# Row maxima of two heads reduced by one VectorE instruction out of two neighbouring PSUM banks, and banks shared out by index

## The chip, the cores and the metric

The kernel runs on one core of a Trainium2 chip. The metric is the time of one execution on the device in microseconds (us); for the kernel before it is the median of three runs. A core has five engines that matter here: TensorE (PE in the profile, with its weight loads as PEld), VectorE (DVE), ScalarE (ACT), GpSimd (POOL) and SyncE (SP), which issues DMAs. Each works off its own queue of instructions in order and waits on semaphores of the others. Matmul results go to PSUM, which has eight banks of 128 partitions by 512 fp32 values; a matmul here fills at most one bank, and the bank can be written again when its last reader is done.

## The reference

One transformer layer in fp32 on 2048 rows of 512, without masking:

```python
# layernorm(x) = (x - mean) / sqrt(var + 1e-5)
qkv = layernorm(x) @ wqkv                 # 512 x 1536, 32 heads of 16
p = softmax(q @ k.T * 16 ** -0.5)         # per head, 2048 x 2048
h = x + (p @ v) @ wo
out = h + silu(layernorm(h) @ w1) @ w2    # w1: 512 x 1792, w2: 1792 x 512
```

## The kernel before, in words

Every large product in it is made of three matmuls with a high and a low part of each factor (`product`, L129 to 136). The 2048 rows of x are four blocks of 512 (`NB`), and attention goes over 32 items (`ITEMS`): one block of queries by four heads. The program has these stages.

1. *Projections by block* (L649 to 693). Each block projects one group of 128 columns of k and of q (`project_qk`), then four tiles of v (`project_v`); layernorm and transposes (`turn_x`) of the next block lie between. The results `ps_qk` are scaled on ScalarE (`ks`, `sh`) with a low part `sl` on VectorE (block 0, L541) or GpSimd (L538); `ps_v` is copied to `va` by ScalarE, and a transpose `ps_tr` is read by ScalarE (`xth`) and then by VectorE (`xtl`).
2. *The rest of the q and k columns* (L717 to 731), 24 products, numbered n from -4 to 19.
3. *Attention* (`scores`, `values`): per group of 128 keys and four heads four score matmuls `ps_s`, four exps on ScalarE (`pt`, L423) and four value matmuls into the bank `pv`. A score that is issued ahead of its stage takes a bank of another kind, as in `begin_scores` (L699) and `some_scores` (L984).
4. After each block of queries its output projection (`output`, L1019) and its MLP (`mlp`, L974): the first product in 14 steps f (L996 to 1005), with SiLU on ScalarE (`g`) and its two halves (`gh`) on ScalarE and GpSimd; then the second (`second`, L954) in 14 steps over four accumulators `ps_acc`, at whose end VectorE adds the residual (`ot`, L971). The last block's is written out apart.

The exponent needs a row maximum for each head and query beforehand. `maximum` (L259) makes a piece of it: one matmul of 128 queries by 512 keys (48 rows deep, as q and k lie there as high and low parts) into a bank, and one VectorE `tensor_reduce` with max to a single column (L271). That is 64 per item and 2048 in all. They are put into the program as fillers. In attention one lies beside each score. Elsewhere they come as bursts (`burst`, L393), in the middle of products: `BESIDE_V`, `BESIDE_V1`, `BESIDE_A` and `BESIDE_A1` give the counts and places in stages 1 and 2; `BESIDE_T` (L712) those of the last two products ahead of attention; `BURSTS_1` has six in most steps of the first MLP product, `BURSTS_2` has 16, 15 and 13 bursts of four in the second; `MORE` puts three beside an output projection, and `last_scores` two behind the last scores. Burst elements alternate between heads with j = 0 and j = 1 (`at["half"]`), which lie on SBUF partitions 0 to 47 and 64 to 111; such matmuls stand on different rows of the PE array, and in the trace the two start 3 to 4 ns apart. The next pair starts 0.22 us later.

All instructions keep the program's order on their engine (`mm`, `pin`, `act`, `dve` and so on). So the order of the work is written by hand, and what a tile framework decides is the semaphores, and, for PSUM, which bank of a pool a tile gets: the pool hands out a bank that has become free. The pools are opened by stage with `open_banks`: sm=5 and st=3 in stage 1 (L428), sm=6, st=1 and su=1 in stage 2 (L714), and from attention on st=4, three pools of one bank that `sm` goes through in a ring, and `pv` (L735). Products take from `st` (stage 2: `st` and `su` by turns), maxima from `sm`. A burst of six in stage 1 takes one more from `st` (L682); a burst in the MLP takes `pv`, which is free there, and in the first product two of `st` (L1004, L1009).

Of the kernel before, what the change touches and what calls it, by code (L numbers as in the profile page):

```python
# [20 lines left out]
P = 128  # L21
# [51 lines left out]
BESIDE_V = [(0, 0), (0, 4, 4, 4)], [(4, 4), (4, 4, 4, 4)], [(6, 6), (6, 6, 6, 5)]  # L73
# [15 lines left out]
def attention_mlp_kernel(ctx: ExitStack, tc: tile.TileContext, x, wqkv, wo, w1, w2, out):  # L89
# [50 lines left out]
    small = ctx.enter_context(tc.tile_pool(name="small", bufs=3))  # L140
    banks = {}

    def open_banks(scope, n, **sizes):

        for kind, bufs in sizes.items():
            banks[kind] = scope.enter_context(tc.tile_pool(name=f"ps_{kind}{n}", bufs=bufs, space=PSUM))

    def bank(name, kind="st", dtype=F32):
        pool_of = banks[kind]
        if isinstance(pool_of, list):  # L150
            pool_of.append(pool_of.pop(0))
            return pool_of[-1].tile([P, 512], dtype, tag=pool_of[-1].name, name=name)
        return pool_of.tile([P, 512], dtype, tag=kind, name=name)
# [50 lines left out]
    def turn(src, dst_h, dst_l, kind="st"):  # L204

        ps = bank("ps_tr", kind).rearrange("p (c n) -> p c n", n=P)
# [52 lines left out]
    def maximum(i, kb, qt, a, j, ps=None):  # L259

        piece = piece_of(i, a)
        n = 1 if i == LAST else 2
        if piece not in mx:
            mx[piece] = small.tile([P, 64], F32, name="mx", bufs=RING + 1)[:, :32 * n].rearrange(
                "p (j a q k) -> p j a q k", j=2, a=n, k=4)
            left[piece] = 32 * n
        if ps is None:
            ps = bank("ps_m", "sm")
        mm(ps, qs[i % RING][64 * j:64 * j + 48, a, qt * P:qt * P + P],
           ks[i % RING][64 * j:64 * j + 48, a, kb * 512:kb * 512 + 512], start=True, stop=True)  # L270
        pin(nc.vector.tensor_reduce(mx[piece][:, j, a % n, qt, kb:kb + 1], ps, axis=AX.X, op=ALU.max))  # L271
        left[piece] -= 1
        return left[piece] == 0
# [31 lines left out]
    def place_max(piece):  # L305

        i, a = piece
        ns = split.pop(piece)
        n = ns.shape[1]
        ps = bank("ps_n", "sm", F16)  # L310
# [47 lines left out]
    def one_max(half=None, ps=None):  # L358

        i = next_item()  # L360
        if i == ITEMS:
            return
        if half is None:
            half = at["half"]
            at["half"] = 1 - half
        if at["blocks"]:

            i = min(range(2), key=lambda n: (todo[n, half] or todo[n, 1 - half] or [(n, KC)])[0][1])
        elif not todo[i, half] and 64 * (i + 2) <= at["ready"] and KC * i - at["next"] > 12:

            i += 1
        half = half if todo[i, half] else 1 - half
        at["done"] += 1
        block = todo[i, half].pop(0)
        piece = piece_of(i, block[3])
        found_all = maximum(*block, ps)

        finish_rest()
        if found_all:
            steps = due_at(piece)  # L380
            g = at["group"]
            if g is None or g + 1 in marks:
                soon(steps, place_max, piece)
                finish_max(piece, g is not None)
                return
            late.setdefault(at["step"] + steps, []).append(piece)
            if steps == WAIT:
                unfinished.append(piece)
                found_at["step"] = at["step"]
            else:  # L390
                finish_max(piece, False)

    def burst(n, *more):  # L393
        for ps in more:
            one_max(ps=ps)
        for _ in range(n - len(more)):
            one_max()
# [16 lines left out]
    def scores(g, k, kind="st"):  # L414

        i = g // KC
        a, j, c = head(g, k)
        assert piece_of(i, a) in placed
        ps = bank("ps_s", kind)
        mm(ps, ks[i % RING][64 * j:64 * j + 64, a, c * P:(c + 1) * P], qs[i % RING][64 * j:64 * j + 64, a, :],  # L420
           start=True, stop=True)
        pts[g, k] = pt_tile("pt")
        act("activation", pts[g, k], ps, AF.Exp, scale=qk_f)  # L423


    with ExitStack() as pa:
        pb = pa.enter_context(ExitStack())
        open_banks(pb, 0, sm=5, st=3)  # L428
# [46 lines left out]
        def measure_rest():  # L475
            n = sum(PIECES)
            ps = bank("ps_sq", "sm")
# [31 lines left out]
        def measure(meanwhile):  # L509

            ps = bank("ps_sq")
# [11 lines left out]
        def project_qk(b, n, beside={}, scale=False, kind="st"):  # L523
# [3 lines left out]
            ps = bank("ps_qk", kind)  # L527
# [19 lines left out]
        def project_v(b, t):  # L547
            ps = bank("ps_v")
# [22 lines left out]
        def idle(n):  # L571
            ps = bank("ps_i")
# [3 lines left out]
        def turn_high(b, t):  # L576
            ps = bank("ps_tr", "sm").rearrange("p (c n) -> p c n", n=P)
# [13 lines left out]
        def first_products(t, *chunks):  # L591
            if t == len(ps_vs):
                ps_vs.append(bank("ps_v", "st" if t < 3 else "sm"))
# [120 lines left out]
        open_banks(pa, 1, sm=6, st=1, su=1)  # L714

        pools.append(ctx.enter_context(tc.tile_pool(name="bp0", bufs=EARLY, side="right")))
        for g in range(1, NG // 2):  # L717
            for m, (b, key) in enumerate([(b, 1) for b in range(NB)] + [(b, 0) for b in range(NB)]):
# [10 lines left out]
                project_qk(b, 2 * g + key, beside, True, "su" if n % 2 else "st")  # L729
# [74 lines left out]
    def divide_part(part, pvs, o_t, kind="st"):  # L804
        ps = bank("ps_q", kind).rearrange("p (t n) -> p t n", n=P)
# [12 lines left out]
    def turn_part(part, o_t, kind="st", engine="act"):  # L818
        ps = bank("ps_o", kind)
# [134 lines left out]
    def second(b, acc, f, gh, gl, inserts={}):  # L954
        w2h, w2l = ws.pop(("w2", f))
        while f == 0 and len(acc) < 4:
            acc.append(bank("ps_acc"))
# [16 lines left out]
    def mlp(b):  # L974
# [13 lines left out]
        def last_scores():  # L988
# [3 lines left out]
            if b < 2:  # L992
                burst(2)

        gates = []
        for f in range(FC):  # L996
# [3 lines left out]
            ps = bank("ps_w1")  # L1000
# [3 lines left out]
                  {6: lambda: burst(n, pv, bank("ps_m"), bank("ps_m"))} if n else {})  # L1004
# [4 lines left out]
        inserts = {SPAN_2 * (n + 1) // BURSTS_2[b]: lambda: burst(4, pv) for n in range(BURSTS_2[b])}  # L1009
# [9 lines left out]
    def output(b, n):  # L1019

        if n < 4:
            ps = bank("ps_wo")
            weave(project_rows(n, ps), {6: lambda: burst(3)} if n < MORE[b] else {})
# [29 lines left out]
    def finish_last(pending):  # L1053
# [5 lines left out]
        ps_rows = [bank("ps_wo", "sm") for _ in range(3)] + [bank("ps_wo")]  # L1059
# [14 lines left out]
        begun = [bank("ps_w1") for _ in range(3)]  # L1074
# [9 lines left out]
        def turn_first(t):  # L1084
            ps = bank("ps_tr", "sm").rearrange("p (c n) -> p c n", n=P)
# [48 lines left out]
        for f in range(FC):  # L1134
# [5 lines left out]
            else:  # L1140
                ps = bank("ps_w", "sm")
# [137 lines left out]
```

## Time and profile before

| what | value |
|---|---|
| median of three runs | 1619.38 us (1619.26 to 1620.99) |
| profiled execution | 1619.58 us |
| its span in the profile | 1617.8 us |
| granted PE clock | 1.00 in every stretch |
| VectorE reduces of `maximum` | 1971 out of `ps_m` and 77 out of `pv` |
| exps | 2048, 609 ns each |

The profile is one execution. A row of the timeline has start and length in us, engine, line of the kernel, operation, output and inputs by the program's names with their shape and type, how many like instructions were put together (x5), and in square brackets the idle time of the engine before it and what ended that. When several instructions are put together, the length runs from the first start to the last end. A row of a group has busy time and mean length in ns, and then the idle time ahead of the group. A row of the chain of waits has start, length and the engine and line that the end hung on. In the table of stretches the columns are the stretch, its length, then busy time and instructions of PE, PEld, DVE, ACT and POOL, the granted clock and the share of the DMA engines.

### The profile page before, as it was taken

Reading aid. Unit: us, or ns where it says so; the run is one execution under the profiler, and the core shown is the slowest. Engines: PE = TensorE matmul, PEld = TensorE weight load, DVE = VectorE, ACT = ScalarE, POOL = GpSimd, SP = SyncE. Lnnn points to the kernel's source line nnn. Section 1 sums busy time; section 2 is a strip of 40 time slices with the busy share of each in tenths; the row PEclk is TensorE's granted clock in tenths of the full one; section 3 lists DMA queues with packets and bytes.
Section 4 is the critical chain, followed back from the end, with each engine's and each line's share of the span. In section 5 each row is a group of like instructions: output and inputs, shape, how many; then the busy total and the mean of one; then the engine's idle time right before and its main releaser. Section 6 shows DMA issues by size and latency. Waiting matters only on the chain.

```text
span 1617.8 us, 28583 instructions
## 1 busy us (share of the span) xinstructions
PE 1603.5 (99%) x10553; PEld 516.2 (32%) x10553; DVE 1408.8 (87%) x2340; ACT 1208.0 (75%) x2397; POOL 443.8 (27%) x696
## 2 busy tenths in 40 slices
PE   9999999999999999999999999999999999999998
PEld 7666422222233322222233322222233322222253
DVE  7899999999998889999998889999987789998421
ACT  5545699999973169999973169999974189999732
POOL 4423455454435201121135201121126101211200
PEclk9999999999999999999999999999999999999999
DMA  5657433334333111111133211111133111100222
GB/s 200 178 160 219 128 98 95 100 113 118 94 76 95 63 51 33 38 45 48 47 77 93 66 51 33 37 49 44 46 78 98 60 51 36 34 12 22 72 85 72
DMA packets 100952, 125.91 MB, mean 78 GB/s; under 512 B 24144, under 2 KB 61072, under 8 KB 100812
## 3 DMA queue, kind: packets, MB, share of 16 engines
q1 hardware_dynamic: 96204, 115.71, 25.4%
q10 hardware_dynamic: 4608, 8.39, 1.9%
q8 instruction: 82, 1.34, 0.3%
q14 instruction: 58, 0.48, 0.1%
HBM read 93.45 MB, written 24.63 MB: 73 GB/s over the span
## 4 chain that ended last, share of the span: by engine, by line
PE 90%; DVE 6%; ACT 3%; issue 1%; DMA 0%; POOL 0%; SPq 0%; DVEq 0%; ACTq 0%
PE pv L96 30%; PE ps_s L96 22%; PE ps_m L96 10%; PE ps_acc L96 9%; PE ps_w L96 8%; PE ps_qk L96 5%; DVE mx L271 4%; ACT pt L110 3%; PE ps_v L96 3%; PE ps_wo L96 2%; PE ps_tr L99 1%; DVE st L113 0%; PE ps_n L99 0%; DVE ot L113 0%; DVE pvs L113 0%
## 5 line engine op out<-in xcount | busy, mean ns | idle before, releaser
L271 DVE TENSOR_REDUCE mx<-ps_m 128x1 f32<-128x512 f32 x1971 | 1233.1, 683 | 51.5 <-PE ps_m L96 21.8
L110 ACT ACTIVATE pt<-ps_s 128x512 f32<-128x512 f32 x2048 | 1010.5, 609 | 152.3 <-PE ps_s L96 133.0
L96 PE MATMUL pv<-pt,va 128*17 128x512 f32 x4096 | 537.5, 598 | 0.6
L96 PE MATMUL ps_s<-qs,ks 64*128 64x512 f16 x2048 | 532.5, 379 | 2.2 <-ACT pt L110 0.5
L96 PE MATMUL ps_m<-ks,qs 48*128 48x512 f16 x1971 | 496.5, 380 | 0.6 <-DVE mx L271 0.2
L96 PEld LDWEIGHTS <-ks 64*128 64x128 f16 x2048 | 149.8, 95 | 548.6 <-issue 434.8
L103 POOL TENSOR_TENSOR ri<-rc,minus 128x16 f32<-128x16 f32 x31 | 90.7, 2927 | 264.4 <-DMA rc<-dn 264.4
L96 PE MATMUL ps_acc<-w,gh 128*128 128x512 f16 x672 | 157.2, 380 | 0.0
L96 PEld LDWEIGHTS pv<-pt,va 128*17 128x17 f32 x4096 | 68.9, 95 | 215.9 <-issue 203.0
L96 PEld LDWEIGHTS <-qs 48*128 48x128 f16 x2048 | 118.7, 94 | 59.6 <-issue 49.2
L110 ACT ACTIVATE g<-ps_w,factors 128x512 f32<-128x512 f32 x56 | 38.5, 687 | 127.6 <-PE ps_w L96 123.3
L96 PE MATMUL ps_w<-hth,w 128*128 128x512 f16 (+1 forms) x472 | 132.9, 369 | 0.0
L96 PEld LDWEIGHTS <-w 128*128 128x128 f16 x708 | 66.2, 98 | 87.9 <-issue 20.8
L96 PEld LDWEIGHTS <-gh 128*128 128x128 f16 x672 | 61.1, 98 | 90.9 <-issue 25.0
L271 DVE TENSOR_REDUCE mx<-pv 128x1 f32<-128x512 f32 x77 | 52.9, 687 | 42.6 <-PE ps_m L96 41.2
L103 POOL TENSOR_TENSOR mx<-mx 128x32 f32<-128x32 f32 x40 | 9.7, 241 | 282.6 <-DVE mx L271 280.8
L96 PE MATMUL ps_w<-htl,w 128*128 128x512 f16 (+1 forms) x236 | 83.9, 368 | 0.0
L103 POOL TENSOR_SCALAR nm<-nm 128x16 f32<-128x16 f32 (+1 forms) x53 | 13.5, 254 | 175.3 <-DVE nm L282 147.8
L110 ACT ACTIVATE ks<-ps_qk,qk_s 128x512 f32<-128x512 f32 x30 | 20.7, 689 | 53.6 <-PE ps_qk L96 51.7
L113 DVE SCALAR_TENSOR_TENSOR gh<-g,factors,gh 128x512 f16<-128x512 f32 x14 | 10.5, 752 | 52.1 <-ACT gh L110 52.1
L103 POOL TENSOR_TENSOR sl<-ks,sh 128x512 f16<-128x512 f32 x30 | 34.8, 1161 | 72.0 <-ACT sh L110 55.6
L96 PE MATMUL ps_qk<-xth,wqk_h 128*128 128x512 f32 x128 | 53.6, 419 | 0.0
(132 smaller groups left out, 1043.1 us busy)
## 6 DMA issues: line engine op xcount, KB each, us to landing
ks<-kd SPq DMA_DIRECT2D x120, 192.0 KB
w<-w1d SPq DMA_DIRECT2D x56, 256.0 KB
w<-w2d SPq DMA_DIRECT2D x56, 256.0 KB
ks<-in_B_w_dram ACTq DMA_DIRECT2D x28, 256.0 KB
w<-in_B_w_dram SPq DMA_DIRECT2D x28, 256.0 KB
qs<-qd SPq DMA_DIRECT2D x128, 48.0 KB
kd<-sh SPq DMA_DIRECT2D x16, 256.0 KB
qd<-sh SPq DMA_DIRECT2D x16, 256.0 KB
```

The costliest lines, as they stand in the source:

```text
L96: tc.keep_in_program_order(nc.tensor.matmul(*a, **k))
L99: tc.keep_in_program_order(nc.tensor.transpose(*a))
L103: tc.keep_in_program_order(getattr(nc.gpsimd, op)(*a, **k))
L110: pin(getattr(nc.scalar, fn)(*a, **k))
L113: pin(getattr(nc.vector, fn)(*a, **k))
L271: pin(nc.vector.tensor_reduce(mx[piece][:, j, a % n, qt, kb:kb + 1], ps, axis=AX.X, op=ALU.max))
```

## The change

PSUM becomes one tile of eight banks, and rings of bank numbers take the place of the pools: `bank` gives the next number of a ring, whether its last user is done or not. `lay_out` sets the rings and starts them anew. The kinds are sm = 0 to 4 and st = 5 to 7 in block 0; from block 1 through stage 2 sm = 0 to 5 and st = 6, 7; in attention st = 0 to 3, sm = 4, 5, 7 and `pv` = 6. The first MLP product alternates between banks 0 and 1, the second has its accumulators in 0 to 3.

In a burst the two heads j = 0 and j = 1 of the same keys, queries and a go into two neighbouring banks, and one `tensor_reduce` reads both: 128x2 out of 128x1024 instead of twice 128x1 out of 128x512. In the MLP the pairs are banks (4, 5), (6, 7) and (2, 3) by turns of a burst, or the first two; elsewhere the next even number of `sm` with its successor. Where no such two are left, two singles are made (6 times). Beside scores, beside the output projection and behind the last scores maxima stay single. 288 reduces are pairs. The last burst of `BESIDE_V` has six instead of five, so that one maximum fewer is left for attention. The matmuls, the instructions of ScalarE and GpSimd and the DMA issues stay the same in number and order, but for some maxima in attention that stand one place further on.

```diff
-BESIDE_V = ... [(6, 6), (6, 6, 6, 5)]
+BESIDE_V = ... [(6, 6), (6, 6, 6, 6)]
...
+    space = psum.tile([P, 8, 512], F32, name="ps")
...
+    def lay_out(**rings):
+        for kind, ring in rings.items():
+            banks[kind] = list(ring)
+    def next_bank(kind):
+        ring = banks[kind]
+        ring.append(ring.pop(0))
+        return ring[-1]
+    def next_pair(kind="sm"):
+        n = next_bank(kind)
+        if n % 2:
+            n = next_bank(kind)
+        assert next_bank(kind) == n + 1
+        return n
+    def bank(kind="st", dtype=F32):
+        ps = space[:, next_bank(kind), :]
+        return ps if dtype == F32 else ps.bitcast(dtype)[:, :512]
...
+        heads = (0, 1) if j is None else (j,)
+        for m, h in enumerate(heads):
+            mm(space[:, n + m, :], qs[i % RING][64 * h:64 * h + 48, a, qt * P:qt * P + P],
+               ks[i % RING][64 * h:64 * h + 48, a, kb * 512:kb * 512 + 512], start=True, stop=True)
+        of = mx[piece][:, :, a % width, qt, kb]
+        if j is None:
+            pin(nc.vector.tensor_reduce(of, space[:, n:n + 2, :], axis=AX.X, op=ALU.max))
+        else:
+            pin(nc.vector.tensor_reduce(of[:, j:j + 1], space[:, n, :], axis=AX.X, op=ALU.max))
...
+    def burst(n, *pairs):
+        for m in range(n // 2):
+            two_max(pairs[m] if pairs else next_pair())
...
-        open_banks(pb, 0, sm=5, st=3)
+        lay_out(sm=range(5), st=range(5, 8))
...
+            if b == 1:
+                lay_out(sm=range(6), st=range(6, 8))
...
-                    n_max = BESIDE_V[b - 1][kind == "v"][n - 2 if kind == "v" else n]
-                    burst(n_max, *[bank("ps_m")] * (n_max > 5))
+                    burst(BESIDE_V[b - 1][kind == "v"][n - 2 if kind == "v" else n])
...
-        open_banks(pa, 1, sm=6, st=1, su=1)
...
-                project_qk(b, 2 * g + key, beside, True, "su" if n % 2 else "st")
+                project_qk(b, 2 * g + key, beside, True)
...
-    open_banks(ctx, 2, st=4, m0=1, m1=1, pv=1, m2=1)
-    banks["sm"] = [banks.pop(f"m{n}") for n in range(3)]
-    pv = bank("pv", "pv")
+    lay_out(st=range(4), sm=(4, 5, 7))
+    pv = space[:, 6, :]
...
             if b < 2:
-                burst(2)
+                singles(2)
 
         gates = []
+        lay_out(st=range(4))
...
-            ps = bank("ps_w1")
+            ps = space[:, f % 2, :]
...
-                  {6: lambda: burst(n, pv, bank("ps_m"), bank("ps_m"))} if n else {})
+                  {6: lambda: burst(n, 4, 6, 2)} if n else {})
...
-        inserts = {SPAN_2 * (n + 1) // BURSTS_2[b]: lambda: burst(4, pv) for n in range(BURSTS_2[b])}
+        inserts = {SPAN_2 * (n + 1) // BURSTS_2[b]: lambda: burst(4, 4, 6) for n in range(BURSTS_2[b])}
...
-            weave(project_rows(n, ps), {6: lambda: burst(3)} if n < MORE[b] else {})
+            weave(project_rows(n, ps), {6: lambda: singles(3)} if n < MORE[b] else {})
```

`two_max` (new) finds the next keys, queries and a that both heads still lack and calls `maximum` with j = None and the pair's first bank.

More of the change, by code (lines that the diff above doesn't have):

```diff
@@ L140, in attention_mlp_kernel @@
     small = ctx.enter_context(tc.tile_pool(name="small", bufs=3))
+    psum = ctx.enter_context(tc.tile_pool(name="psum", bufs=1, space=PSUM))
+    space = psum.tile([P, 8, 512], F32, name="ps")
     banks = {}
[L143 to L153, printed above, removed]
+    def lay_out(**rings):
[14 more added lines that the diff above has]
+        return ps if dtype == F32 else ps.bitcast(dtype)[:, :512]
     ident = const.tile([P, P], F32, name="ident")
@@ L204, in turn @@
     def turn(src, dst_h, dst_l, kind="st"):
-        ps = bank("ps_tr", kind).rearrange("p (c n) -> p c n", n=P)
+        ps = bank(kind).rearrange("p (c n) -> p c n", n=P)
         for c in range(4):
@@ L257, in attention_mlp_kernel, with maximum @@
     mx, left = {}, {}
-    def maximum(i, kb, qt, a, j, ps=None):
+    def maximum(i, kb, qt, a, j, n):
         piece = piece_of(i, a)
-        n = 1 if i == LAST else 2
+        width = 1 if i == LAST else 2
         if piece not in mx:
[L264 to L273, printed above, removed]
+            mx[piece] = small.tile([P, 64], F32, name="mx", bufs=RING + 1)[:, :32 * width].rearrange(
+                "p (j a q k) -> p j a q k", j=2, a=width, k=4)
+            left[piece] = 32 * width
+        heads = (0, 1) if j is None else (j,)
[7 more added lines that the diff above has]
+            pin(nc.vector.tensor_reduce(of[:, j:j + 1], space[:, n, :], axis=AX.X, op=ALU.max))
+        left[piece] -= len(heads)
+        at["done"] += len(heads)
+        finish_rest()
+        if left[piece] == 0:
+            found_maxima(piece)
     def finish_max(piece, urgent):
@@ L356, in due_at, with found_maxima, one_max @@
         return joint - g if joint < start_of(piece) - 2 and joint // KC - 1 not in (-1, *FIRSTS) else WAIT
-    def one_max(half=None, ps=None):
+    def found_maxima(piece):
+        steps = due_at(piece)
+        g = at["group"]
+        if g is None or g + 1 in marks:
+            soon(steps, place_max, piece)
+            finish_max(piece, g is not None)
+            return
+        late.setdefault(at["step"] + steps, []).append(piece)
+        if steps == WAIT:
+            unfinished.append(piece)
+            found_at["step"] = at["step"]
+        else:
+            finish_max(piece, False)
+    def one_max(half=None, n=None):
         i = next_item()
@@ L372, in one_max, with two_max, singles @@
         half = half if todo[i, half] else 1 - half
[L373 to L396, printed above, removed]
+        maximum(*todo[i, half].pop(0), next_bank("sm") if n is None else n)
+    def two_max(n):
+        i = next_item()
+        if i == ITEMS:
+            return
+        both = [next(((t[1], m, t) for t in todo[m, 0] if (*t[:4], 1) in todo[m, 1]), None)
+                for m in (range(2) if at["blocks"] else (i,))]
+        both = min((x for x in both if x), default=None)
+        if both is None:
+            one_max(n=n)
+            one_max(n=n + 1)
+            return
+        _, i, t = both
+        for j in range(2):
+            todo[i, j].remove((*t[:4], j))
+        maximum(*t[:4], None, n)
+    def burst(n, *pairs):
+        assert n % 2 == 0
+        for m in range(n // 2):
+            two_max(pairs[m] if pairs else next_pair())
+    def singles(n):
+        for _ in range(n):
             one_max()
@@ L476, in measure_rest @@
             n = sum(PIECES)
-            ps = bank("ps_sq", "sm")
+            ps = bank("sm")
             mm(ps[:, :n + DC], ones, rest_sq, start=True, stop=True)
@@ L509, in measure @@
         def measure(meanwhile):
-            ps = bank("ps_sq")
+            ps = bank()
             mm(ps[:, :NG], ones, sq, start=True, stop=True)
@@ L571, in idle @@
         def idle(n):
-            ps = bank("ps_i")
+            ps = bank()
             for c in range(n):
@@ L576, in turn_high @@
         def turn_high(b, t):
-            ps = bank("ps_tr", "sm").rearrange("p (c n) -> p c n", n=P)
+            ps = bank("sm").rearrange("p (c n) -> p c n", n=P)
             for c in range(4):
@@ L592, in first_products @@
             if t == len(ps_vs):
-                ps_vs.append(bank("ps_v", "st" if t < 3 else "sm"))
+                ps_vs.append(bank("st" if t < 3 else "sm"))
             for c in chunks:
@@ L1058, in finish_last @@
         act("activation", small.tile([P, 1], F32, name="sw"), ident[:, :1], AF.Silu)
-        ps_rows = [bank("ps_wo", "sm") for _ in range(3)] + [bank("ps_wo")]
+        ps_rows = [bank("sm") for _ in range(3)] + [bank()]
         first = [project_rows(t, ps_rows[t], range(3), stop=False) for t in range(4)]
@@ L1073, in finish_last @@
         found, parts = {}, {}
-        begun = [bank("ps_w1") for _ in range(3)]
+        begun = [bank() for _ in range(3)]
         def add(t):
@@ L1084, in turn_first @@
         def turn_first(t):
-            ps = bank("ps_tr", "sm").rearrange("p (c n) -> p c n", n=P)
+            ps = bank("sm").rearrange("p (c n) -> p c n", n=P)
             for c in range(4):
@@ L1140, in finish_last @@
             else:
-                ps = bank("ps_w", "sm")
+                ps = bank("sm")
                 w1h, w1l = (w.rearrange("p (c n) -> p c n", n=P) for w in ws["w1", f])
```

20 lines of the change are left out of this document (10 added, 10 removed).

## The prediction

> **What bounds the kernel now.** First the page: its busy line, its chain by engine, and the group that the change touches.
>
> ```profile
> PE 1603.5 (99%) x10553; PEld 516.2 (32%) x10553; DVE 1408.8 (87%) x2340; ACT 1208.0 (75%) x2397; POOL 443.8 (27%) x696
> PE 90%; DVE 6%; ACT 3%; issue 1%; DMA 0%; POOL 0%; SPq 0%; DVEq 0%; ACTq 0%
> L271 DVE TENSOR_REDUCE mx<-ps_m 128x1 f32<-128x512 f32 x1971 | 1233.1, 683 | 51.5 <-PE ps_m L96 21.8
> ```
>
> TensorE (PE) is never without work for long, and the maxima on VectorE (DVE) reach the chain only in places. The table of stretches says where: in attention, here 190 to 430 us, ScalarE (ACT) is as full as PE, and VectorE has 10 us to spare.
>
> ```profile
> 190.00:430.00 240.00, 239.51 (x1828) 53.70 (x1826) 229.56 (x373) 239.85 (x490) 116.56 (x166) 1.00 0.39 109
> ```
>
> The change leaves the attention maxima single, so a lighter VectorE buys nothing there. What remains is the stretches beside it, read matmul by matmul. In the first product of the MLP a burst of six maxima comes every 12 matmuls; the timeline shows the first of a run, the second, and the next two:
>
> ```profile
> 487.00 0.39 PE L96 MATMUL pv<-ks,qs 48*128 48x512 f16 x1
> 487.01 0.82 PE L96 MATMUL ps_m<-ks,qs 48*128 48x512 f16 x5
> 487.43 0.69 DVE L271 TENSOR_REDUCE mx<-pv 128x1 f32<-128x512 f32 x1 [1.43 <-PE ps_m L96]
> 488.03 3.07 DVE L271 TENSOR_REDUCE mx<-ps_m 128x1 f32<-128x512 f32 x5
> 490.45 0.39 PE L96 MATMUL pv<-ks,qs 48*128 48x512 f16 x1
> 490.46 1.07 PE L96 MATMUL ps_m<-ks,qs 48*128 48x512 f16 x5
> 494.16 0.39 PE L96 MATMUL pv<-ks,qs 48*128 48x512 f16 x1
> 497.75 0.39 PE L96 MATMUL pv<-ks,qs 48*128 48x512 f16 x1
> ...
> 876.34 20.42 DVE mx L271 x34
> ```
>
> Bursts start 3.45 us apart as long as nothing waits (487.00 to 490.45), then 3.71 and 3.59: the last maximum of a burst waits for a bank that VectorE still reads (1.07 against 0.82 us for the same five matmuls). The last row, from the chain of waits, is the same run of the second MLP: 20.42/34 = 0.60 us from one reduce to the next, and six of them are 3.60. VectorE sets the pace of these runs, by 0.14 us a burst.
>
> **The change part by part.** *One pair's reduce.* No row has 1024 elements, so I bound it: two single reduces take 1.20 from start to start, the dearest case. The cheapest bound has slope alone: a small reduce out of PSUM is
>
> ```profile
> L113 DVE TENSOR_REDUCE qk_s<-ps_sq 128x1 f32<-128x8 f32 x1 | 0.2, 167 | 1.0 <-PE ps_sq L96 1.0
> ```
>
> so 504 more elements cost 683 − 167 = 516 ns, 1.024 ns each. Twice 512 then is 683 + 524 = 1.21 us long; a reduce's start comes 0.08 before its predecessor's end (0.683 against 0.60), so 1.13 apart. An element cost without any fixed part gives 1.05. I take 1.13, which rests on two rows of the same instruction. The Trainium skill, "Perfetto Trace Analysis", section "Optimizing Scalar/DVE Operations", states some 125 ns of overhead per DVE instruction on PSUM and that grouping helps a saturated engine; by it (an estimate) a pair would be 1.20 − 0.125 = 1.07 and the total 1.2 us lower than mine. No run before shows a pair, so I leave it out of the sum.
>
> *Gains.* Six maxima now take 3 × 1.13 = 3.39 of the 3.45. A run of six bursts lost 0.26 + 4 × 0.14 = 0.82; four such runs (two in each of the first two MLPs) lose 3.3. Of that I leave 0.09 at every second burst, since the third pair's bank comes free 0.43 + 2 × 1.13 + 1.21 = 3.90 after a burst's start (0.43 is 487.00 to 487.43), and is wanted at 3.45 + 0.43 (0.82 − 0.39, the last start of the five): with 0.04 for the handover, which is what the reduce at 487.43 took after its matmul's end, about 0.07 to 0.09. **−2.2**. The third MLP has three pairs of bursts with the 0.26 and one 0.22 more: **−0.75**. In the second product every burst of four that follows closely pays the same way:
>
> ```profile
> 549.32 0.74 PE L96 MATMUL ps_m<-ks,qs 48*128 48x512 f16 x3
> 552.05 0.60 PE L96 MATMUL ps_m<-ks,qs 48*128 48x512 f16 x3
> ...
> 101.35 1.10 PE L96 MATMUL ps_m<-ks,qs 48*128 48x512 f16 x6
> ```
>
> 0.14 each, 8 times in the first MLP and 5 in the second, less a tenth to a fifth: **−1.55**. The start of the second projection phase (the last row: 1.10 where six matmuls else take 0.82, then three bursts with 0.12) gives **−0.6**. Gains: 5.1. The 288 reduces that vanish elsewhere lie behind a busy PE and give nothing: VectorE's share falls, the span doesn't.
>
> *Losses: the rings.* A pool gave the bank that was free; a ring gives the next by index. Instruction for instruction PE's order is kept, so I put after's bank numbers on before's times and looked where a bank's last reader ends after the matmul that now wants it. Between projections the ring `st` has two banks where the pool had three.
>
> ```profile
> 28.59 0.39 PE L96 MATMUL ps_qk<-xth,wqk_h 128*128 128x512 f32 x1
> 29.51 0.75 DVE L113 SCALAR_TENSOR_TENSOR sl<-ps_qk,qk_s,sh 128x512 f16<-128x512 f32 x1 [1.06 <-ACT sh L110]
> ...
> 33.55 1.16 POOL L103 TENSOR_TENSOR sl<-ks,sh 128x512 f16<-128x512 f32 x1
> 34.39 0.48 PE L96 MATMUL ps_v<-wv_h,xth 128*128 128x512 f32 x1
> 34.75 0.69 ACT L110 ACTIVATE ks<-ps_qk,qk_s 128x512 f32<-128x512 f32 x1 [1.90 <-POOL sl L103]
> 37.44 0.59 ACT L110 COPY va<-ps_v 128x512 f32<-128x512 f32 x1 [0.34 <-PE ps_v L96]
> 37.59 0.48 PE L96 MATMUL ps_v<-wv_h,xth 128*128 128x512 f32 x1
> ...
> 59.83 1.06 PE L96 MATMUL ps_m<-ks,qs 48*128 48x512 f16 x4
> 60.82 0.66 PE L99 MATMUL ps_tr<-ident,ks 128*128 128x128 f32 x4
> 60.98 0.68 DVE L113 TENSOR_TENSOR xtl<-ps_tr,xth 128x512 fp32r<-128x512 f32 x1
> ```
>
> (1) At 28.59 block 1 begins in bank 6, which block 0 has just filled; VectorE's `sl` reads it till 30.26: **+1.7** with the handover. Behind it on PE stands everything. (2) At 34.39 the first `ps_v` gets bank 7 and waits for ACT's `ks`, to 35.44, itself behind POOL's `sl`; PE is 1.7 late by then, POOL about 1.0, so **+0.6**. (3) At 37.59 the next one waits for ACT's `va`, to 38.03: **+0.5**. (4) At 60.82 a transpose waits for `xtl` of the transpose before, to 61.66: +0.9, less the 0.45 that the burst at 59.83 no longer waits (1.06 against 0.60): **+0.5**. From 40 to 190 us PE has no idle time to absorb these.
>
> (5) Ahead of attention a pair takes banks 4 and 5, and 5 holds a score that ACT has not yet read:
>
> ```profile
> 185.04 0.44 PE L96 MATMUL ps_m<-ks,qs 48*128 48x512 f16 x2
> 185.84 1.08 ACT L110 ACTIVATE pt<-ps_s 128x512 f32<-128x512 f32 x2
> ```
>
> An exp takes 0.6 (two overlap in the 1.08), so the first ends at 186.45; the second matmul of the row above, 0.05 behind its twin (0.44 − 0.39), goes then instead of at 185.09: **+1.4**. (6) The second product's accumulators are the banks 0 to 3 now, where bank 1 holds the last gate:
>
> ```profile
> 534.06 1.68 PE L96 MATMUL ps_acc<-w,gh 128*128 128x512 f16 x7
> 534.06 0.69 ACT L110 ACTIVATE g<-ps_w,factors 128x512 f32<-128x512 f32 x1 [1.15 <-PE ps_w L96]
> 899.55 1.24 PE L96 MATMUL ps_acc<-w,gh 128*128 128x512 f16 x5
> 899.81 0.69 ACT L110 ACTIVATE g<-ps_w,factors 128x512 f32<-128x512 f32 x1 [2.09 <-POOL gh L103]
> 1257.67 3.07 DVE L271 TENSOR_REDUCE mx<-ps_m 128x1 f32<-128x512 f32 x5
> 1258.70 1.89 PE L96 MATMUL ps_acc<-w,gh 128*128 128x512 f16 x8
> 1258.96 0.69 ACT L110 ACTIVATE g<-ps_w,factors 128x512 f32<-128x512 f32 x1 [2.01 <-PE ps_w L96]
> ```
>
> The second accumulator starts three matmuls after the first, 0.64 by (1.24 − 0.39)/4 each, so it waits for ACT's end at 534.75, 900.50 and 1259.65: 0.1, 0.35 and 0.35; in the third the next accumulator's bank 2 waits for the last of three pairs too, which ends 6 × 0.60 − 3 × 1.13 = 0.2 before the six singles do, at 1260.5 instead of 1257.67 + 3.07, and some 0.2 after it is wanted (1258.70 + 6 × 0.21 + the 0.35): **+1.0**. (7) Where attention resumes, a score's bank waits for the residual of the last accumulator:
>
> ```profile
> 949.24 2.26 ACT L110 ACTIVATE pt<-ps_s 128x512 f32<-128x512 f32 x4
> 949.51 0.40 PE L96 MATMUL ps_s<-qs,ks 64*128 64x512 f16 x2
> 949.59 0.74 DVE L113 SCALAR_TENSOR_TENSOR ot<-ps_acc,factors,ot 128x512 f32<-128x512 f32 x1
> ```
>
> 0.8 us, three times. ACT works on four exps till 951.50 there, so the score has time and most is hidden; I charge 0.2 each, and nothing for the scores of the last product: **+0.5**. Uncovered it would be 2.4.
>
> Losses: 1.7 + 0.6 + 0.5 + 0.5 + 1.4 + 1.0 + 0.5 = 6.2. One more maximum ahead of attention and one fewer in it moves no bound: nothing. ACT's, POOL's and SP's orders, and with them every DMA issue, are as before. Sum: 6.2 − 5.1 = +1.1. The profiled execution took 1619.58 (span 1617.80, 1.78 around it), 0.2 above the median of the runs, so **1620.5** beside the median of 1619.4.
>
> **The rivals.**
> *A, forecast*: both halves as worked out. Its own range is 1618 to 1622.6: the sum with the cheapest pair (1.05 to 1.07) and half of wait 5 hidden, up to waits 7 uncovered.
> *B, slower: a pair costs what two singles cost.* At 1.20 three pairs are 3.60, the third pair's bank is free at 0.43 + 2.40 + 1.28 = 4.1, and a run of bursts loses 0.14 or more each as before; the second product's pairs end 2.9 after their start where bank 6 is wanted at 2.82. Gains fall to 0.5: 1619.4 + 6.2 − 0.5 = **1625**. It decides from about 1.16 on; each 0.01 over 1.13 returns some 0.6 us. For it: a bank is held 1.21 where it was held 0.68. Against: 167 ns for eight elements. The Trainium skill, "Perfetto Trace Analysis", section "Optimizing Scalar/DVE Operations", says that an engine which isn't saturated but makes others wait may do better with smaller instructions; by it the bursts lose, which is this rival, and wait 6 of the third MLP is the one place where my sum has that.
> *C, faster: the early waits don't reach the end.* Waits 1 to 3 and 5 (4.2 us) would be made up if PE met waits in 40 to 190 us that end at a fixed time, such as a load, or if ACT still caught up in the start of attention. Then 1620.5 − 4.2 = **1616**. Speaks for: ACT waits 1.90 for POOL at 34.75, so some slack exists. Against: no DMA is in the chain, 0%.
> *D, it isn't done*: pairs fall back on singles. The order of after has 288 reduces fewer and 6 pairs split, so this is small; the time would be that of B.
>
> **How the numbers follow.** A 0.58, B 0.22, C 0.17, D 0.03. A measurement tells 0.2%, 3.2 us, from no change: 1616.1 to 1622.6. Faster: half of C and a little of A, 0.12. Slower: B and D, and the upper tail of A, 0.28. Same: 0.60. The range of 1616.0 to 1625.0 holds A, C's nearer half and B up to its own value.
>
> **What would show it.** The pair's row, 128x2 out of 128x1024: about 1.21 us, 1.13 from one to the next (B: over 1.25). VectorE 1408.8 less 288 × 0.07 (by spacing) to 0.16 (by length), some 1375 us; PE's idle time in the MLP's first products nearly gone, their bursts 3.45 apart. Against that, new gaps on PE at 28.6, 34, 37.6 and 185, with the releasers named above, and each later event shifted by their sum: attention should begin some 4 us later, and the MLPs win about 1.7, 1.2 and 0 back. If the shift at 180 is under 1 us, C is right; if the MLPs win nothing, B is. The forecast fails as a whole if a pair's two matmuls no longer run side by side, 0.22 us each 288 times, which nothing here suggests.

## The result, and the profile after

The changed kernel takes 1622.22 us (median of 17 runs, 1621.98 to 1623.64) against 1619.38 before (17 runs). The ratio is 1.0018 with a 95% interval of 1.001 to 1.0025, so it is 2.8 us slower, just inside the 0.2% that the prediction called no change. The profiled spans differ by the same amount, 1620.6 less 1617.8.

From the page of the kernel after: the busy line, the chain by engine, and the two groups of reduces.

```profile
PE 1600.2 (99%) x10553; PEld 521.3 (32%) x10553; DVE 1392.9 (86%) x2052; ACT 1207.9 (75%) x2397; POOL 442.6 (27%) x696
PE 90%; DVE 5%; ACT 3%; issue 1%; DMA 0%; POOL 0%; SPq 0%; DVEq 0%; ACTq 0%
L287 DVE TENSOR_REDUCE mx<-ps 128x1 f32<-128x512 f32 x1472 | 926.5, 684 | 47.0 <-PE ps L96 18.8
L285 DVE TENSOR_REDUCE mx<-ps 128x2 f32<-128x1024 f32 x288 | 336.1, 1220 | 62.0 <-PE ps L96 61.3
```

A pair takes 1.22 us. VectorE has 15.9 us less work. PE is "busy" 3.3 us less, and that is no gain: matmuls of 0.39 us start 0.22 apart, so the short stalls of before lay under the length of the matmul ahead of them and counted as busy, while the new waits are longer and show as idle time. The page as a whole tells almost nothing of what happened. The view of PE's waits does (what waits, for whom; us in total, times, longest). Of these six releasers the view of the kernel before has only `pt`, with three waits of 0.5 us in all:

```profile
PE ps L96 <- DVE sl L113: 1.6, 1, 1.6
...
PE ps L96 <- DVE ot L113: 1.3, 3, 0.5
PE ps L96 <- ACT pt L110: 1.2, 1, 1.2
...
PE ps L99 <- DVE xtl L113: 0.9, 1, 0.9
...
PE ps L96 <- ACT ks L110: 0.5, 1, 0.5
...
PE ps L96 <- ACT g L110: 0.4, 2, 0.2
```

Those for `sl`, `pt`, `xtl` and `ks` come once each, ahead of attention, those for `ot` at the blocks' ends and those for `g` in the MLPs. (Three waits for `htl`, 0.8 in all, are new too, but the matmuls behind them are as late as those ahead, so they cost nothing.) The timeline of after has the early ones one by one, with one for `va` besides; set each beside the same matmul of before (28.59, 34.39, 37.59, 60.82 and 185.11 us):

```profile
30.68 0.51 PE L96 MATMUL ps<-xth,wqk_h 128*128 128x512 f32 x1 [1.56 <-DVE sl L113]
37.38 0.50 PE L96 MATMUL ps<-wv_h,xth 128*128 128x512 f32 x1 [0.49 <-ACT ks L110]
41.07 0.50 PE L96 MATMUL ps<-wv_h,xth 128*128 128x512 f32 x1 [0.24 <-ACT va L110]
64.88 0.66 PE L99 MATMUL ps<-ident,ks 128*128 128x128 f32 x4 [0.91 <-DVE xtl L113]
190.20 0.37 PE L96 MATMUL ps<-ks,qs 48*128 48x512 f16 x1 [1.21 <-ACT pt L110]
```

The bracket is shorter than the delay, since it counts only from the end of the matmul before; the difference of the starts is what PE lost. Because both kernels run the same matmuls, such a difference can be followed through the whole program, and it is the account of the change. In the table a positive number means that after is later at that matmul.

| matmul | before, us | after, us | later by | step |
|---|---|---|---|---|
| second transpose of block 0 | 8.43 | 8.77 | 0.35 | 0.35, a load of x |
| block 1, first `ps_qk` | 28.59 | 30.68 | 2.09 | 1.73, wait 1 |
| first `ps_v` | 34.39 | 37.38 | 2.99 | 0.73 wait 2, 0.17 ahead of it |
| second `ps_v` | 37.59 | 41.07 | 3.48 | 0.5, wait 3 |
| transpose | 60.82 | 64.88 | 4.07 | 0.57, wait 4, net |
| burst in phase 2 | 116.12 | 119.46 | 3.34 | -0.2 made up at 65.3; -0.5, gain |
| first product behind the pair | 185.41 | 190.50 | 5.09 | 0.2 on the way, 1.6 wait 5 |
| first MLP, first burst | 487.01 | 492.10 | 5.09 | attention: nothing |
| its first accumulator | 534.06 | 538.18 | 4.12 | -1.0, gain |
| its end, a score | 589.58 | 593.46 | 3.88 | -0.65, gain; 0.24, a score behind a pair; 0.18, wait 7 |
| second MLP, first accumulator | 899.55 | 902.34 | 2.79 | -1.0, gain; -0.1, a transpose |
| its end, a score | 953.92 | 956.63 | 2.72 | 0.35, wait 6; -0.5, gain; -0.1; 0.18, wait 7 |
| third MLP, first accumulator | 1258.70 | 1260.86 | 2.15 | -0.6, gain |
| its first burst of four | 1261.17 | 1263.94 | 2.77 | 0.6, wait 6 |
| near the end | 1612.78 | 1615.59 | 2.82 | 0.19, wait 7; -0.14 elsewhere |

The gains are where they were looked for. Bursts of the first MLP product in after, with VectorE's reduces:

```profile
492.10 0.82 PE L96 MATMUL ps<-ks,qs 48*128 48x512 f16 x6
494.80 5.95 DVE L285 TENSOR_REDUCE mx<-ps 128x2 f32<-128x1024 f32 x5
495.55 0.92 PE L96 MATMUL ps<-ks,qs 48*128 48x512 f16 x6
499.10 0.82 PE L96 MATMUL ps<-ks,qs 48*128 48x512 f16 x6
...
898.32 2.35 DVE L285 TENSOR_REDUCE mx<-ps 128x2 f32<-128x1024 f32 x2
```

Only every second burst stalls, by 0.10 us (0.92 against 0.82, 3.55 us to the next instead of 3.45); in the kernel before, the second of a run stalled by 0.26 and each later one by 0.14. The last row gives the spacing of pairs: 2.35 − 1.22 = 1.13 us (the row of five takes in the short pauses between bursts).

### The profile page after: what moved, and what is told of

It reads as the page before. It is cut to its first block, busy times and chain, and to the rows that moved or that the text cites. A ratio compares the mean times of both kernels' runs of the same rounds, so it can differ in the third digit from the quotient of the medians.

```text
span 1620.6 us, 28289 instructions
## 1 busy us (share of the span) xinstructions
PE 1600.2 (99%) x10553; PEld 521.3 (32%) x10553; DVE 1392.9 (86%) x2052; ACT 1207.9 (75%) x2397; POOL 442.6 (27%) x696
## 4 chain that ended last, share of the span: by engine, by line
PE 90%; DVE 5%; ACT 3%; issue 1%; DMA 0%; POOL 0%; SPq 0%; DVEq 0%; ACTq 0%
PE ps L96 88%; ACT pt L110 3%; DVE mx L285 2%; DVE mx L287 2%; PE ps L99 1%; DVE ot L113 1%; DVE st L113 0%; DMA ks<-in_A_x_dram 0%; DVE pvs L113 0%; DVE htl L113 0%; DVE hx L113 0%; ACT ks L110 0%; ACT sh L110 0%; POOL rs L103 0%; DVE ks L113 0%
## 5 line engine op out<-in xcount | busy, mean ns | idle before, releaser
L110 ACT ACTIVATE pt<-ps 128x512 f32<-128x512 f32 x2048 | 1010.5, 609 | 152.7 <-PE ps L96 151.0
L287 DVE TENSOR_REDUCE mx<-ps 128x1 f32<-128x512 f32 x1472 | 926.5, 684 | 47.0 <-PE ps L96 18.8
L96 PE MATMUL ps<-pt,va 128*17 128x512 f32 x4096 | 537.5, 598 | 0.6
L96 PE MATMUL ps<-qs,ks 64*128 64x512 f16 x2048 | 532.9, 380 | 3.7 <-DVE ot L113 1.3
L96 PE MATMUL ps<-ks,qs 48*128 48x512 f16 x2048 | 493.3, 381 | 1.6 <-ACT pt L110 1.2
L285 DVE TENSOR_REDUCE mx<-ps 128x2 f32<-128x1024 f32 x288 | 336.1, 1220 | 62.0 <-PE ps L96 61.3
L96 PE MATMUL ps<-w,gh 128*128 128x512 f16 x672 | 157.8, 380 | 0.5 <-ACT g L110 0.4
L96 PEld LDWEIGHTS ps<-pt,va 128*17 128x17 f32 x4096 | 69.1, 95 | 214.7 <-issue 201.6
L96 PE MATMUL ps<-hth,w 128*128 128x512 f16 (+1 forms) x472 | 133.0, 369 | 0.0
L96 PE MATMUL ps<-htl,w 128*128 128x512 f16 (+1 forms) x236 | 84.1, 369 | 0.0
```

The lines of the kernel that those rows point to most:

```text
L96: tc.keep_in_program_order(nc.tensor.matmul(*a, **k))
L110: pin(getattr(nc.scalar, fn)(*a, **k))
L285: pin(nc.vector.tensor_reduce(of, space[:, n:n + 2, :], axis=AX.X, op=ALU.max))
L287: pin(nc.vector.tensor_reduce(of[:, j:j + 1], space[:, n, :], axis=AX.X, op=ALU.max))
```

## The experiments

**One: four product banks for blocks 1 and 2.**

```diff
-                lay_out(sm=range(6), st=range(6, 8))
+                lay_out(sm=range(4), st=(4, 7, 5, 6))
+            if b == 3:
+                lay_out(sm=range(6), st=range(6, 8))
```

> Blocks 1 and 2 get four banks for products (st = 4, 7, 5, 6) and four for maxima; block 3 and all that follows as in the changed kernel. Theory (the loss is made by bank waits of the two-bank ring ahead of 62 us): the four gaps at 28.6, 34, 37.6 and 61 us go, 1.7 + 0.7 + 0.5 + 0.6 = 3.5 us, and the stall of 0.45 of the kernel before at 59.8 does not come back; attention starts 3.5 us earlier and the time is about 1618.7. Rival (these delays are made up before attention, whose start is set by something else): the gaps go, but attention starts as late as before this edit, time about 1622.

Measured: 1618.68 us, 3.5 less than the changed kernel; ratio to before 0.9997 (0.9988 to 1.0006). The same matmul as at 28.59 us starts at 28.61, the one at 60.82 only 0.4 later than in before. Attention is entered 1.4 us later than in before instead of 5.1, and the 3.5 us reach the end. Waits 1 to 4 are worth what the matmuls' starts say. The rival is out.

**Two: the pair ahead of attention ten matmuls later.**

```diff
-{1: lambda: (begin_scores(2), burst(2))}
+{1: lambda: begin_scores(2), 11: lambda: burst(2)}
```

> The pair of maxima in the last product ahead of attention is put behind its eleventh matmul instead of its first; nothing else differs from the changed kernel. Theory (the pair's second bank holds a score whose exp has not run): the gap of 1.6 us at 188.6 goes, attention starts that much earlier, time about 1620.7. Rival (ACT is the bound there, so that the wait is hidden and only moves): no change, 1622.2.

Measured: 1621.46 us, 0.8 less: half of what the theory gave. The gap of wait 5 is gone, but attention is entered 4.0 us later than in before, where the changed kernel is 4.7 later (both less what their first load brought): 0.8 of the 1.6 came back. The timeline shows why:

```profile
191.34 1.23 DVE L285 TENSOR_REDUCE mx<-ps 128x2 f32<-128x1024 f32 x1 [1.74 <-PE ps L96]
192.61 0.40 PE L96 MATMUL ps<-ks,qs 48*128 48x512 f16 x2 [0.60 <-DVE mx L285]
```

The first maximum of attention takes bank 4, which the pair now still fills. It isn't ScalarE that hides part of the wait; the edit made a new wait of the same kind. Behind the eighth matmul (experiment six) some 0.3 is left, as a score still waits for the pair's reduce:

```profile
188.33 0.37 PE L96 MATMUL ps<-qs,ks 64*128 64x512 f16 x1 [0.22 <-DVE mx L285]
```

**Three: the same banks, but two single reduces for each pair.**

```diff
-            two_max(pairs[m] if pairs else next_pair())
+            first = pairs[m] if pairs else next_pair()
+            one_max(n=first)
+            one_max(n=first + 1)
```

> The same banks and the same matmuls as the changed kernel, but each pair is read by two single reduces (2340 VectorE instructions with a result in the profile again). Theory (the pair's cheaper reduce, 1.14 instead of 1.20 from start to start, gives what the MLPs and the second projection phase win): the first products' bursts go back to 3.59 us apart in their runs, the win of 2.6 us there and of 1.2 us in the second products goes, and 0.6 at the start of the second projection phase, time 1625.5 to 1626.5. Rival (the win comes from which banks the bursts use, not from the pairs): the bursts keep a mean of 3.50 and the time stays within 1622 to 1623.

Measured: 1626.45 us, ratio to before 1.0045 (1.0031 to 1.0059), 4.2 us above the changed kernel. The bursts go back to their old pace:

```profile
492.30 0.82 PE L96 MATMUL ps<-ks,qs 48*128 48x512 f16 x6
492.72 11.45 DVE L287 TENSOR_REDUCE mx<-ps 128x1 f32<-128x512 f32 x19 [1.43 <-PE ps L96]
495.75 1.08 PE L96 MATMUL ps<-ks,qs 48*128 48x512 f16 x6
499.45 0.96 PE L96 MATMUL ps<-ks,qs 48*128 48x512 f16 x6
503.04 0.96 PE L96 MATMUL ps<-ks,qs 48*128 48x512 f16 x6
```

Nineteen reduces at (11.45 − 0.68)/18 = 0.598 us, and bursts 3.59 apart. So the layout by index alone (with the sixth maximum) costs about 7 us, and the pairs give 4.2 of it back. The gain is the pairs', not the banks'.

**Four: the two-bank ring in the other order.**

```diff
-                lay_out(sm=range(6), st=range(6, 8))
+                lay_out(sm=range(6), st=(7, 6))
```

> Only the order of the two-bank ring differs from the changed kernel: it begins with bank 7 instead of bank 6. Theory (each gap is a wait for that bank's own last reader, so that the ring's phase decides the first): the gap of 1.7 at 28.6 us goes; the one at 34.4 gets longer, to about 1.1, since ScalarE's and GpSimd's work does not move as far as PE's; the other two stay: attention 1.3 to 1.7 us earlier, time 1620.5 to 1621. Rival (two banks are too few in any order): the wait moves on to the next product in full, and the time stays at 1622.

Measured: 1620.43 us, 1.8 less. Wait 1 is gone, and wait 2 grew as expected, to 1.1 us from start to start:

```profile
35.32 0.69 ACT L110 ACTIVATE ks<-ps,qk_s 128x512 f32<-128x512 f32 x1 [1.90 <-POOL sl L103]
36.06 0.50 PE L96 MATMUL ps<-wv_h,xth 128*128 128x512 f32 x1 [0.86 <-ACT ks L110]
```

ScalarE waits 1.90 for GpSimd again, just as in before. In the changed kernel this read 1.53: with PE late, part of that wait had been absorbed. Waits in a row aren't independent: 0.4 of what wait 1 had cost went to wait 2, and 0.2 came back at wait 5.

**Five: the accumulators in another order.**

```diff
-        lay_out(st=range(4))
+        lay_out(st=(0, 2, 3, 1))
...
-                  {6: lambda: burst(n, 4, 6, 2)} if n else {})
+                  {6: lambda: burst(n, *((2, 4, 6) if f == 13 else (4, 6, 2)))} if n else {})
```

> The changed kernel with the second product's accumulators in the order of banks 0, 2, 3, 1, and the last burst of the third MLP's first product in the order (2, 3), (4, 5), (6, 7). Theory (the second accumulator waits for the last SiLU out of bank 1, in the third MLP also for the last pair out of 2 and 3): the waits of 0.1, 0.3 and 0.6 us at the start of the second products go, time about 1621.2. Rival (the next step waits for the same SiLU's product anyway): 1622.2.

Measured: 1621.7 us (1620.88 to 1623.95), 0.5 less, in runs that scatter more than the others. The median of the times doesn't tell 0.5 from 1.0, since in some of the long runs the excess lies outside the program's span (the run of 1623.95 has a span of 1619.0). The medians of the spans do, 1619.0 against 1620.1. So does the profile: the eleven matmuls up to the first burst run without a break, where the changed kernel's third MLP has three and then eight:

```profile
1259.78 2.54 PE L96 MATMUL ps<-w,gh 128*128 128x512 f16 x11
```

```profile
1260.86 0.81 PE L96 MATMUL ps<-w,gh 128*128 128x512 f16 x3
1261.12 0.69 ACT L110 ACTIVATE g<-ps,factors 128x512 f32<-128x512 f32 x1 [2.01 <-PE ps L96]
...
1261.85 2.16 PE L96 MATMUL ps<-w,gh 128*128 128x512 f16 x8 [0.19 <-ACT g L110]
```

The first fence is the experiment's timeline, the second that of after: the fourth matmul, the second accumulator's first, waits for the SiLU that ends at 1261.81.

**Six: all of it.** Experiments one and five, and the pair behind the eighth matmul.

```diff
-{1: lambda: (begin_scores(2), burst(2))}
+{1: lambda: begin_scores(2), 8: lambda: burst(2)}
```

> Pairs with none of the six waits: four product banks in blocks 1 and 2, the accumulators as in the run before this one, and the pair ahead of attention behind the eighth matmul of its product, where both its banks have been read and its reduce ends ahead of the first score of attention. Theory (gains and losses add up): 3.5 + 1.5 + 1.0 less than the changed kernel, about 1616.3, 0.19% below the kernel before. Rival (part of wait 5 is ScalarE's own, as when the pair stood behind the eleventh matmul and 0.9 of the 1.6 us came back): about 1617.

Measured: 1616.43 us, ratio to before 0.9982 (0.9973 to 0.9991). That is 5.8 us less than the changed kernel, where 6.0 were expected from the waits' sizes; the 0.3 left of wait 5 covers the difference.

**Seven: and the blocks' ends.**

```diff
+        if b < 3:
+            banks["st"] = [2, 3, 0, 1]
```

> As the run before this one, and at the end of each MLP the ring st goes on with banks 2, 3, 0, 1, so that the bank whose residual VectorE adds last is taken last. Theory (the score at the block's end waits for that residual, and ScalarE runs dry behind it): 0.3 + 0.2 + 0.1 less, about 1615.7. Rival (ScalarE has scores enough): the same as the run before.

Measured: 1615.81 us, 0.6 less; ratio to before 0.9979 (0.997 to 0.9988). Two lines of after, the score of the block's end and the reader of its bank, show what was mended:

```profile
588.73 0.74 DVE L113 SCALAR_TENSOR_TENSOR ot<-ps,factors,ot 128x512 f32<-128x512 f32 x1
...
589.52 0.37 PE L96 MATMUL ps<-qs,ks 64*128 64x512 f16 x1 [0.49 <-DVE ot L113]
```

The view of PE's waits has no `sl`, `xtl`, `va`, `g`, `pt` or ScalarE's `ks` left. Of `ot` two waits of 0.5 us in all remain, where the changed kernel has three of 1.3. The waits for pairs have grown from one to three: one of 0.23 at 60.6 us comes with the shorter ring of maxima banks, and one of 0.22 at 188.4 is what is left of wait 5.

```profile
PE ps L96 <- DVE mx L285: 0.9, 3, 0.4
...
PE ps L96 <- DVE ot L113: 0.5, 2, 0.3
```

**Eight: five maxima again in the last burst of the blocks** (two pairs and a single).

```diff
+                    if (b, n) == (3, 5):
+                        burst(4)
+                        singles(1)
```

> The changed kernel with five maxima in the last burst of the blocks again (two pairs and a single), so that one more is left for attention. Theory (attention is bound by ScalarE, one maximum more or less moves no end): 1622.2 within 0.3. Rival (the sixth maximum delays the second projection phase by its 0.2 us of PE): 1622.0 or less.

Measured: 1621.28 us, 0.9 less: more than either had. Followed by the starts of matmuls and set against after's own first load, 0.25 us come by the start of the second projection phase. The rival had this size, but it isn't PE's time for the sixth maximum: that matmul runs beside its twin, and the burst takes 0.82 us with five as with six. VectorE's reduce of the pair is longer than that of a single, and the next burst waits for it. First after, then the experiment:

```profile
98.15 0.82 PE L96 MATMUL ps<-ks,qs 48*128 48x512 f16 x6
101.44 1.08 PE L96 MATMUL ps<-ks,qs 48*128 48x512 f16 x6
```

```profile
97.26 0.82 PE L96 MATMUL ps<-ks,qs 48*128 48x512 f16 x5
100.50 0.82 PE L96 MATMUL ps<-ks,qs 48*128 48x512 f16 x6
```

Another 0.6 come in one step in the last step of the second MLP's first product, where a transpose of finished maxima (`place_max`) stands. Again first after, then the experiment:

```profile
898.32 2.35 DVE L285 TENSOR_REDUCE mx<-ps 128x2 f32<-128x1024 f32 x2
...
899.59 0.21 PE L99 MATMUL ps<-ident_h,ns 128*32 128x128 f16 x1 [0.53 <-DVE mx L285]
```

```profile
897.00 1.22 DVE L285 TENSOR_REDUCE mx<-ps 128x2 f32<-128x1024 f32 x1
...
897.68 0.23 PE L99 MATMUL ps<-ident_h,ns 128*32 128x128 f16 x1
```

By the program, the transpose lies in bank 7 in after, where the pair (6, 7) is still read till 899.54, and in bank 4 in the experiment. One single more or less ahead of this point turns the ring of three by one. The turn also moves a wait of 0.4 us of a score for a pair from the end of the first MLP to that of the third.

Neither of the two waits is a loss against the kernel before, which has both, behind singles:

```profile
97.87 0.82 PE L96 MATMUL ps_m<-ks,qs 48*128 48x512 f16 x6 [0.25 <-DVE mx L271]
896.80 0.22 PE L99 MATMUL ps_n<-ident_h,ns 128*32 128x128 f16 x1 [0.62 <-DVE mx L271]
```

**Nine: only the ring's phase.**

```diff
-    lay_out(st=range(4), sm=(4, 5, 7))
+    lay_out(st=range(4), sm=(5, 7, 4))
```

> The changed kernel, with the ring of maxima banks from attention on begun at bank 5 instead of bank 4 (5, 7, 4); six maxima in the blocks' last burst as in the changed kernel. The run with five there was 0.9 us faster, of which the profile puts 0.6 at one transpose of maxima in the second MLP (899.6 us in the changed kernel), which lies in bank 7 under a pair still being read there, and in bank 4 with five. Theory (the phase of the ring, which one single more or less shifts, decides that wait): the wait goes here too, time about 1621.6. Rival (it was the maximum taken out): 1622.2.

Measured: 1621.91 us (1621.48 to 1624.18), 0.3 less, between the two. In the profile the wait is gone, as the theory has it: from the last first-product step to the first burst of the second MLP the lag falls by 0.3 where it rises by 0.3 in after. But the profiled execution lost 1.5 us elsewhere, at the start of attention, and to nothing in the program (last section). The median neither proves nor refutes 0.6; the place of the wait is shown, and its worth is shown by experiment eight's profile and the next run.

**Ten: the version that follows from all of it**, experiments seven and eight together.

> The run with all six waits and the block ends mended (1615.8), and five maxima in the blocks' last burst again. Theory (0.2 us of PE in the second projection phase's start and the transpose's wait of 0.6 are paid by the sixth maximum): about 1615.0. Rival (the 0.9 us was scatter between executions' first loads): 1615.8.

Measured: 1615.25 us (1614.86 to 1615.48), ratio to before 0.9974 (0.9964 to 0.9984), 0.56 less than without the five. It is 4.1 us faster than the kernel before and 7.0 faster than the change as it was made. About 0.6 of the 4.1 is the transpose's wait, which the kernel before has too.

## Why the prediction came out as it did

The forecast was no change, 1620.5 us; 1622.22 was measured, inside its range and 1.7 above it. The range was 9 us wide, and the time still counts as no change by only 0.4 us. Every gain and wait of the sum was found where it was put; the sizes were off, nearly all to the slower side, so little cancelled.

- *The pair's reduce*: 1.21 long and 1.13 apart were predicted from the slope between two rows, 1.22 and 1.13 to 1.14 measured. By spacing a pair saves 2 × 0.598 − 1.14 = 0.06 us, by length 2 × 0.684 − 1.22 = 0.15. VectorE's busy time fell by what the spacing gives (288 × 0.06 = 17 against 15.9), not to 1375. The Trainium skill's "Perfetto Trace Analysis", section "Optimizing Scalar/DVE Operations", has 125 ns of overhead for each such instruction; half of that was saved here by spacing, and it is the spacing that the bursts feel.
- *Gains*: 5.1 predicted, 4.3 by the matmuls' starts and 4.2 by experiment three. Short were the second products, 1.2 instead of 1.55, since the second pair of every second burst still waits 0.04 us, and the third MLP's first product, 0.6 instead of 0.75 for the same reason at 0.10. The first products of the first two MLPs gave 2.0 of the 2.2, the second projection phase 0.5 of the 0.6.
- *Losses*: 6.2 predicted, 7.0 found. Waits 1, 3, 4 and 6 were right within 0.1 (1.73, 0.5, 0.57, 0.97). Wait 2 came to 0.73 with 0.17 just ahead of it, against 0.6, and wait 5 to 1.6 against 1.4: the exp that it waits for, 185.84 us in before and 189.56 in after, was 0.2 later than PE was. Another 0.2 came between 116 and 185 us, for which the prediction had no term. Wait 7 was charged 0.5 and cost 0.18, 0.18 and 0.19; experiment seven gives 0.6 for it. A score at the end of the first MLP waits for a pair's reduce, 0.24, without a term in the prediction; 0.1 came back at the ends of each of the other two.
- *What is left over*: 0.8 of gains and 0.8 of losses, less the 0.2 made up at 65.3, make 1.4 of the 1.7. The other 0.3 lies outside the program's span: the runs of after take 2.1 us around it (median), those of the kernel before 1.8, for which the prediction had no term. Why isn't known. Single executions differ besides: the first load comes between 0.5 earlier and 0.6 later than in before in the profiled ones.
- *One more maximum ahead of attention "moves no bound: nothing"* was wrong: with five the changed kernel is 0.9 us faster (experiment eight), 0.25 by a burst's wait for VectorE and 0.6 by the turn of the ring, a thing that the prediction didn't think of. This is time that the change failed to win, not part of the 2.8 us that it lost, since the kernel before has both waits.
- *The rivals*: B's rule, that smaller instructions do better where an engine isn't saturated, is refuted for the bursts by experiment three, and its price, 1.20 us for a pair, by the 1.13. C, that the early waits are made up, is refuted by experiment one; only 0.2 was made up, at 65.3 us, where the kernel before waits for ScalarE's `va` and after comes later than it. D was not so: 288 pairs are in the profile.

The change moved the time little because it was two changes of opposite sign. Pairs are worth 4 us, and giving banks out by index costs 7, of which 6.4 went by other sizes and orders of the rings and another place for one pair (experiments six and seven).

## What to carry to other kernels

When banks (or any buffers) are given out in a fixed order instead of by what is free, look for the last reader of each bank at every place where the ring's size, start or phase changes; one allocation more or less turns the ring for all that follows. Since the order of matmuls was the same in both kernels, the difference of starts of the same matmul shows every wait with its worth, while busy shares show nothing (99% both times). Merging two reduces paid only where a matmul waits for a bank that a reduce still reads: here in the bursts of six, whose single reduces need 3.60 us of a 3.45 us period, and in bursts of four that follow closely (2.59 us apart), whose last bank came free 0.14 us late although four reduces need only 2.40.

## What the runs showed of the hardware that was not expected

In the profiled execution of experiment nine the granted PE clock fell to half for some 3.4 us, 1.2 us behind the gap of wait 5. The table of stretches has the clock third from the end; what it lacks to 1.00 in three of them, 0.68, 1.00 and 0.04 us, is half of 3.4, of which 1.4 lies ahead of 192.00:

```profile
188.00:190.00 2.00, 0.79 (x3) 0.27 (x2) 1.24 (x3) 1.83 (x4) 0.99 (x1) 1.00 0.11 35
190.00:192.00 2.00, 2.00 (x7) 1.57 (x7) 1.83 (x6) 0.00 (x0) 0.17 (x1) 0.66 0.49 165
192.00:194.00 2.00, 2.00 (x7) 1.07 (x8) 0.20 (x1) 0.00 (x0) 0.00 (x0) 0.50 0.08 16
194.00:196.00 2.00, 1.72 (x16) 0.34 (x15) 1.40 (x3) 1.82 (x4) 0.39 (x1) 0.98 0.00 0
```

Three matmuls of that execution's timeline, the pair's behind the gap, one still at full length and one behind that:

```profile
189.43 0.37 PE L96 MATMUL ps<-ks,qs 48*128 48x512 f16 x1 [1.21 <-ACT pt L110]
...
190.30 0.40 PE L96 MATMUL ps<-xth,wqk_h 128*128 128x512 f32 x1
...
191.28 0.63 PE L96 MATMUL ps<-xth,wqk_h 128*128 128x512 f32 x1
```

In the profile of after, PE is idle about as long at the same place (1.00 us busy of the two from 188 to 190), and the clock stays at 1.00. Seven profiled executions have this gap, of 1.00 to 1.21 us; one of them lost 1.5 us behind it, and that the gap was the cause isn't shown. The Trainium skill's "TensorE: Matmul & The Clock Gate", section "What's actually happening", has the clock at half after an idle window of some 3.4 us; the half agrees with the 0.50 here, but the idle time ahead of it was the 1.21 us in the bracket of the pair's matmul, far below that window. The runs without a profile don't settle it: those of 1.4 to 2.3 us above their median are from kernels that keep wait 5 (the changed kernel and experiments five, eight and nine), but the kernel before, which doesn't have that gap, has one 1.6 above.
